# Converting float64 weights on the chip: a shift and an integer addition become one shift-and-or

## The chip, the core and the metric

The kernel runs on one core of one Trainium2 chip. The metric is the device time of one execution in microseconds, the median of several runs. A core has a matrix engine (TensorE, PE in the profile; its weight loads are PEld), a vector engine (VectorE, DVE), an activation engine (ScalarE, ACT), GpSimd (POOL), and queues that issue transfers (SyncE, SP). Each engine works through its own list of instructions in order and waits on semaphores for the others.

## The reference

Block-causal attention, then two two-layer networks, all in float32, with the networks' weights given in float64 (they come out of numpy's generator and are never cast):

```python
scores = scale * np.matmul(q, k.transpose(0, 1, 3, 2))       # 4 x 8 heads, 576 x 64
scores = np.where(block_i >= block_j, scores, -1000000000.0) # blocks of 64
scores = scores - np.max(scores, axis=-1, keepdims=True)
attn = np.exp(scores)
attn = attn / (np.sum(attn, axis=-1, keepdims=True) + 1e-09)
x = np.matmul(attn, v)            # reshaped to 2304 tokens x 512

h = x @ w_in                      # 512 -> 2048, first network
x = np.maximum(0.01 * h, h) @ w_out
h = x @ w_in2                     # 512 -> 2048, second network
out = (h * (1.0 / (1.0 + np.exp(-h)))) @ w_out2
```

## The kernel before, in words

**Stages.** The 2304 tokens are six blocks of 384. Block 0's attention comes first, with PE in full float32; then block 0 goes through the first network, again in full float32 (16 steps of a first-layer product, L1440 or L1454, and a second-layer product, L1466). In that stretch the attention of block 1 is woven in (scores L1046, products with the values L989). Blocks 1 to 5 go through the first network with operands split into a high and a low part, three products each (L1445 to L1447, L1474), with the attention of blocks 2 to 5 woven in (scores L1139, L989). The second network works on all tokens with seven products of halves in place of eight (first layer L1712 to L1714, last layer L1875); its operands are sums and differences of quarters, each split into high and low (`split`: high by L378 or L380, low by L389).

**The conversion.** The chip gets the float64 weights as 64-bit words. `convert` (L407) makes 128 x 512 of them into float32; it runs 64 times: 32 times for the first network (`first_weights`, up to about 124 us), 16 times in `first_pair` and 16 times in `last_raw` for the second (about 480 to 673 us). A transfer brings the words into a slot of the tile `raw` (three slots). Then:

- `scaled` (L425, ACT): the upper half word, read as a float32, times 2^-112, which sets the exponent right; into a tile `cy` (two slots).
- `low` (L433 on ACT or L435 on DVE): the lower half word times 2^-29, rounded to a 16-bit integer: the three mantissa bits that the upper half word does not hold. Rounding can give 8, a carry into the fourth bit. It goes into the lower 16 bits of a slot of `cc` (two slots).
- `signed` (L438, DVE): the sign bit into the upper 16 bits of `cc`.
- `shifted` (L442, DVE): `cy` shifted left by three bits, in place.
- `added` (L447, DVE): `cy` plus `cc` as 32-bit integers, into a weight tile (`w`, `l`) or into `cc`.

**What sets the order.** No order is written by hand. `Schedule` (L75) plays the tasks through once when the program is built: each task has an estimated duration on each engine that may take it, a rank (when it is due) and the tasks that it depends on. A free engine takes the ready task with the lowest rank; where two engines may take a task, the one that is free first gets it. The instructions are written out in the order in which the tasks were taken, so any changed duration or dependency can move instructions on every engine. A conversion's tasks have one rank each, and are released by the load (`t_load`) and the slots of `cy` and `cc`.

**Other lines that the text names.** L1337 to L1387 are block 0's softmax (L1366 the row maximum, L1371 the exponential, L1387 the division), L1393 the transposition of its probabilities on PE, L1344 their product with the values. L1502 is the gate behind a first layer, on ACT. L1149 and L1151 are the row maxima of blocks 2 to 5, L1157 the exponential, L1176 the low part of the probabilities. L1823 to L1833 are the sums for the last layer's operands, whose high and low parts go to `h1` and `l0` among others.

Of the kernel before, what the change touches and what calls it, by code (L numbers as in the profile page):

```python
# [11 lines left out]
I32 = mybir.dt.int32  # L12
U16 = mybir.dt.uint16
U32 = mybir.dt.uint32
I64 = mybir.dt.int64
AF = mybir.ActivationFunctionType
ALU = mybir.AluOpType
# [5 lines left out]
EPS = 1e-09  # L23
PS = 2.0**15
LEAK = 0.01
BLOCKS = (384, 384, 384, 384, 384, 384)
PLACES = (0, 3, 2, 1, 5, 4)
TOK = 256
# [183 lines left out]
def rows_of(t, n):  # L212

    runs = []
    for a in range(t, t + n, P):
        r = PLACES[a // BLOCKS[0]] * BLOCKS[0] + a % BLOCKS[0]
        if runs and sum(runs[-1][1:]) == r:
# [6 lines left out]
def head_ranges(blk, n_heads):  # L224

    pieces = []
    first = t0 = PLACES[blk] * BLOCKS[blk]
    end = first + BLOCKS[blk]
    while t0 < end:
# [10 lines left out]
def attn_mlp_mlp(  # L240
# [10 lines left out]
    nc = tc.nc  # L251
    S, H = SEQ, vL.shape[1]
    D = vL.shape[-1]
    NT, DM = out.shape
    NF = w1.shape[0]
    NC = DM // P
    NJ = (S + P - 1) // P
    NBLK = len(BLOCKS)
    assert sum(BLOCKS) == NT
    NB = max(BLOCKS)  # L260
    NB0 = BLOCKS[0]
    NC0 = NB0 // P
    scale = 1.0 / float(D) ** 0.5
# [61 lines left out]
    def cc_room(dtype):  # L325
        turn_cc[0] = (turn_cc[0] + 1) % CCS
        return area("cc", "c", U32)[:, turn_cc[0] * DM : (turn_cc[0] + 1) * DM].bitcast(dtype)

    def raw_room():

        k = turn_raw[0] = (turn_raw[0] + 1) % RAWS
        return area("raw", turn_raw[1])[:, k * 2 * DM : (k + 1) * 2 * DM]
# [9 lines left out]
    engine = {"DVE": nc.vector, "POOL": nc.gpsimd, "ACT": nc.scalar}  # L342
    plan = Schedule()


    def act(n, psum=False, pointers=0):
        return 0.833 * n + (52 if psum else 94) + 93 * pointers

    def dve(n, pointers=0):
        return Both(1.042 * n + 68 + 61 * pointers)  # L350
# [4 lines left out]
    def dve2x(n, pointers=0):  # L355
        return Both(0.521 * n + 68 + 61 * pointers)
# [10 lines left out]
    def dma(deps, rank, size, emit, issue=600, after=(), slow=0, lag=0):  # L367
        t = plan.add({"SP": issue}, deps, rank, lambda e: emit(), after)
        done = plan.add({"DMA": size / 360}, [t], rank, lambda e: None)
        done.lag = lag  # L370
        if slow:
            done, t0 = plan.add({"LATE": 1}, [done], rank, lambda e: None), done
        done.issue = t
        return done
# [32 lines left out]
    def convert(src, f, sl, rk, load_rank, to=None, slow=0, lag=0):  # L407

        d = {}
        raw_free, raw_after, raw_users = raws.next()
        cy_free, cy_after, cy_users = cys.next()
        cc_free, cc_after, cc_users = ccs.next()

        def load():
            r = raw_room().bitcast(I64)
            nc.sync.dma_start(out=r, in_=src[f, :, sl])
            d["w0"] = r.bitcast(U32).rearrange("p (n two) -> p n two", two=2)[:, :, 0]
            d["sign"] = r.bitcast(U16).rearrange("p (n four) -> p n four", four=4)[:, :, 3]  # L420
            d["top"] = r.bitcast(F32).rearrange("p (n two) -> p n two", two=2)[:, :, 1]

        def scaled(e):
            d["y"] = cy.tile([P, DM], F32, tag="cy", name="cy")
            nc.scalar.activation(d["y"], d["top"], AF.Copy, scale=2.0**-112)  # L425

        def half_words(i):
            return d["c"].bitcast(U16).rearrange("p (n two) -> p n two", two=2)[:, :, i]

        def low(e):  # L430
            d["c"] = cc_room(U32)
            if e == "ACT":
                nc.scalar.activation(half_words(0), d["w0"], AF.Copy, scale=2.0**-29)  # L433
            else:
                nc.vector.tensor_scalar(half_words(0), d["w0"], 2.0**-29, None, op0=ALU.mult)  # L435

        def signed(e):
            nc.vector.tensor_scalar(half_words(1), d["sign"], 0x8000, None, op0=ALU.bitwise_and)  # L438

        def shifted(e):  # L440
            yu = d["y"].bitcast(U32)
            nc.vector.tensor_scalar(yu, yu, 3, None, op0=ALU.logical_shift_left)  # L442

        def added(e):
            ci = d["c"].bitcast(I32)
            d["x"] = d["c"].bitcast(F32) if to is None else to
            engine[e].tensor_tensor(d["x"].bitcast(I32), d["y"].bitcast(I32), ci, op=ALU.add)  # L447

        t_load = dma(raw_free, load_rank, DM * P * 8, load, after=[*raw_after, *raw_later], slow=slow, lag=lag)
        raws.takers.append(t_load.issue)  # L450
        t_y = plan.add({"ACT": act(DM) + 50}, [t_load, *cy_free], rk, scaled, cy_after)
        cys.takers.append(t_y)
        t_w = plan.add({"DVE": dve2x(DM) + 110, "ACT": act(DM) + 150}, [t_load, *cc_free], rk, low, cc_after)
        ccs.takers.append(t_w)
        t_c = plan.add({"DVE": dve2x(DM) + 110}, [t_load], rk, signed, [t_w])
        t_t = plan.add({"DVE": dve2x(DM) + 60}, [t_y], rk, shifted)
        t_x = plan.add({"DVE": dve(DM) + 70}, [t_w, t_c, t_t], rk, added)
        raw_users += [t_y, t_w, t_c]
        cy_users.append(t_x)
        if to is not None:  # L460
            cc_users.append(t_x)
        return d, t_x, cc_users
# [9 lines left out]
    def first_weights():  # L472

        got = []
        for i in range(2 * NF):
            f, sl = i // 2, slice((i % 2) * DM, (i % 2 + 1) * DM)
            rk = CONV0 + CONV1 * f
            to = wx[f][:, sl] if f < NATIVE else None
            got.append(convert(w1, f, sl, rk, LOAD0 + RAW0 + 20 * i if i < 4 else rk - CONV_LOAD, to, slow=LATER if i < 4 else 0))
        return got  # L480
# [102 lines left out]
    def first_pair(p):  # L583

        rk = unit3(0, p) - W2_AHEAD
        d0, t0, users0 = convert(w2, 2 * p, slice(0, DM), rk, rk - CONV_LOAD, lag=LAG)
        d1, t1, users1 = convert(w2, 2 * p + 1, slice(0, DM), rk, rk - CONV_LOAD, lag=LAG)
        t_free, t_after, t_users = cys.next()
        d = {}
# [899 lines left out]
    def add_step(blk, f):  # L1489
# [9 lines left out]
        def gate1(e):  # L1499
            at = (blk * NF + f) % 2 * NB  # L1500
            s.g = gates[0][:, at : at + n]
            nc.scalar.activation(s.g, s.h[:, :n], AF.Prelu, alpha=LEAK)  # L1502

# [561 lines left out]
```

## Time and profile before

| | |
|---|---|
| runs | 912.48, 912.71, 912.92 us; median 912.71 us |
| profiled execution | 912.12 us, span from first to last instruction 910.4 us |
| PE | busy 897.8 us (99%) |
| DVE | busy 781.4 us (86%) |
| ACT | busy 542.6 us (60%) |
| POOL | busy 17.1 us (2%) |
| TensorE clock granted | 1.00 throughout |

The profile is of one execution. Its lines give, for an instruction or a group, the engine, the line of the kernel, what is written and read, the shape, the duration, and in brackets or behind a bar the idle time ahead of it with what ended it. Durations run from start to end; neighbours on DVE and ACT overlap by some 0.05 to 0.1 us, so what an instruction holds its engine for is the distance to its successor's start, called its step here.

### The profile page before, as it was taken

The page shows a single profiled execution, that of the slowest core. Times are in us where ns is not written, and L with a number is a line of the kernel's source. Part 1 is how long each engine was busy: PE and PEld are TensorE (multiplying, and loading weights), DVE is VectorE, ACT ScalarE, POOL GpSimd, SP SyncE. Part 2 cuts the span into 40 slices and gives each one's busy share as a digit, 9 for nine tenths or more (in the row PEclk, how much of TensorE's full clock was granted, in tenths as well). Part 3 has the DMA queues.
Part 4 walks back from the last instruction along what each step waited for, and adds up shares of the span by engine and source line. Part 5 has one row for each costly group of instructions (what it writes and reads, how often), then busy time and mean ns, then how long its engine had stood idle before and what let it go on. Part 6 is the DMA issues. An engine that isn't in the chain of part 4 may idle for free.

```text
span 910.4 us, 18148 instructions
## 1 busy us (share of the span) xinstructions
PE 897.8 (99%) x6569; PEld 832.0 (91%) x6569; DVE 781.4 (86%) x1802; ACT 542.6 (60%) x1195; POOL 17.1 (2%) x79
## 2 busy tenths in 40 slices
PE   9999999999999999999999999999999999999997
PEld 4655569999999999999999999999999999999997
DVE  6889899998898889888828988898899999888865
ACT  7998687776666767676627656564465632131322
POOL 0000000000000000000000000000000000000000
PEclk9999999999999999999999999999999999999999
DMA  7597827766765686856535426688755545353422
GB/s 236 179 236 191 245 89 171 143 147 151 168 162 114 151 161 145 172 157 160 105 95 197 122 82 231 230 292 290 260 192 186 180 125 161 98 159 96 148 67 86
DMA packets 176042, 149.70 MB, mean 164 GB/s; under 512 B 109264, under 2 KB 154064, under 8 KB 175952
## 3 DMA queue, kind: packets, MB, share of 16 engines
q1 hardware_dynamic: 175952, 148.55, 58.9%
q8 instruction: 51, 0.84, 0.4%
q14 instruction: 39, 0.32, 0.1%
HBM read 90.70 MB, written 32.51 MB: 135 GB/s over the span
## 4 chain that ended last, share of the span: by engine, by line
PE 86%; DVE 10%; ACT 2%; issue 1%; DVEq 0%; ACTq 0%
PE acc L1474 12%; PE acc L1875 8%; PE h L1445 5%; PE s L1875 5%; PE h L1446 5%; PE h L1447 5%; PE h L1440 4%; PE s L1139 4%; PE u L1474 4%; PE x L989 3%; PE acc L1466 3%; PE acc L1712 3%; PE acc L1713 3%; PE acc L1714 3%; PE x L1875 3%; PE u L1875 3%
## 5 line engine op out<-in xcount | busy, mean ns | idle before, releaser
L1157 ACT ACTIVATE p<-s,st 128x288 f32<-128x288 f32 (+4 forms) x120 | 62.4, 522 | 44.6 <-DVE st L1149 22.8
L1502 ACT ACTIVATE g<-h 128x384 f32<-128x384 f32 x96 | 46.8, 488 | 55.6 <-PE h L1447 49.0
L1474 PE MATMUL acc<-ghi,w 128*128 128x384 f32 x255 | 66.5, 337 | 0.0
L1139 PE MATMUL s<-k,q 128*128 128x288 f32 (+5 forms) x288 | 65.4, 322 | 0.8 <-ACT p L1157 0.8
L389 DVE TENSOR_TENSOR glo<-g,ghi 128x384 fp32r<-128x384 f32 x80 | 44.2, 552 | 24.4 <-ACT ghi L378 23.8
L1171 ACT ACTIVATE hl<-p,st 128x576 f16<-128x576 f32 (+5 forms) x93 | 55.9, 620 | 15.3 <-DVE st L1167 5.4
L1176 DVE SCALAR_TENSOR_TENSOR hl<-p,st,hl 128x576 f16<-128x576 f32 (+4 forms) x96 | 59.0, 625 | 2.8 <-ACT hl L1171 2.0
L1445 PE MATMUL h<-h,w 128*128 128x384 f32 x180 | 60.7, 337 | 0.0
L1764 ACT ACTIVATE e<-e 128x384 f32<-128x384 f32 (+1 forms) x72 | 42.7, 627 | 27.2 <-DVE e L1737 21.5
L1447 PE MATMUL h<-h,w 128*128 128x384 f32 x160 | 53.6, 335 | 0.0
L1446 PE MATMUL h<-l,w 128*128 128x384 f32 x160 | 53.6, 335 | 0.0
L1139 PEld LDWEIGHTS s<-k,q 128*128 128x128 f32 x288 | 48.0, 188 | 5.1 <-ACT p L1157 1.9
L425 ACT ACTIVATE cy<-raw 128x512 f32<-128x512 f32 x64 | 42.9, 670 | 10.6 <-DVE cc L447 4.9
L1474 PEld LDWEIGHTS acc<-ghi,w 128*128 128x128 f32 x255 | 45.6, 188 | 0.8
L378 ACT ACTIVATE ghi<-g 128x384 fp32r<-128x384 f32 x77 | 40.2, 522 | 1.2
L1474 PE MATMUL acc<-glo,w 128*128 128x384 f32 x120 | 40.2, 335 | 0.0
L1149 DVE TENSOR_REDUCE st<-s 128x1 f32<-128x320 f32 (+3 forms) x72 | 36.4, 505 | 2.4 <-PE s L1139 0.2
L989 PEld LDWEIGHTS <-vp 128*64 128x64 f16 x1296 | 31.5, 111 | 7.2 <-issue 7.2
L1445 PEld LDWEIGHTS h<-h,w 128*128 128x128 f32 x180 | 33.8, 188 | 0.2
L1440 PE MATMUL h<-h,w 128*128 128x384 f32 x96 | 33.8, 495 | 0.0
L378 ACT ACTIVATE h<-raw 128x768 fp32r<-128x768 f32 (+1 forms) x16 | 12.5, 781 | 34.8 <-PE acc L1875 30.6
L1712 PE MATMUL acc<-h,w 128*128 128x384 f32 x96 | 32.2, 335 | 1.0 <-ACT l L378 1.0
(386 smaller groups left out, 2872.1 us busy)
## 6 DMA issues: line engine op xcount, KB each, us to landing
raw<-w SPq DMA_DIRECT2D x64, 512.0 KB, 4.9
raw<-g SPq DMA_DIRECT2D x64, 256.0 KB, 3.1
g<-e SPq DMA_DIRECT2D x48, 192.0 KB, 3.1
g<-e SPq DMA_DIRECT2D x24, 384.0 KB, 3.2
kqr<-kq_l SPq DMA_DIRECT2D x16, 480.0 KB, 3.7
kqr<-kq_l SPq DMA_DIRECT2D x16, 416.0 KB, 3.8
v<-vL SPq DMA_DIRECT2D x16, 320.0 KB, 3.2
y<-yT SPq DMA_DIRECT2D x12, 384.0 KB, 3.9
```

The source lines that it names most:

```text
L989: nc.tensor.matmul(o[i * D : (i + 1) * D, c], v[i][part][:, j], p[i][a], start=start and t == 0, stop=stop and t == len(terms) - 1,)
L1139: nc.tensor.matmul(s[:, :w], hd.q[:, a : a + P], hd.k[:, k0:k1], start=i + j == 0, stop=i == len(hds) - 1 and j == 1,)
L1157: nc.scalar.activation(p[:rows, k0:k1], u.s[piece][:rows, :w], AF.Exp, bias=nm[:rows], accum_out=s2[:rows, piece : piece + 1])
L1171: nc.scalar.activation(hl[:rows, 0, :n], p[:rows], AF.Copy, scale=rc[:rows])
L1176: nc.vector.scalar_tensor_tensor(hl[:rows, 1, :n], p[:rows], rc[:rows], hl[:rows, 0, :n], op0=ALU.mult, op1=ALU.subtract)
L1440: nc.tensor.matmul(h, w[:, c * P : (c + 1) * P], x_hi[0][:, c, : s.n], start=c == 0, stop=c == NC - 1)
L1445: nc.tensor.matmul(h, w1_lo[s.f][:, sl], hi[:, c, : s.n], start=c == 0, stop=False)
L1446: nc.tensor.matmul(h, w1_hi[s.f][:, sl], lo[:, c, : s.n], start=False, stop=False)
L1447: nc.tensor.matmul(h, w1_hi[s.f][:, sl], hi[:, c, : s.n], start=False, stop=c == NC - 1)
L1474: nc.tensor.matmul(s.acc[c][:, : s.n], a, b, start=s.f == 0 and i == 0, stop=s.f == NF - 1 and i == 2)
L1712: nc.tensor.matmul(o, wlo[:, w], xhi[:, x], start=k == 0, stop=False)
L1875: nc.tensor.matmul(o, a[:, x], b, start=i == 0 and j == 0 and q == 0, stop=i == NP - 1 and q == 2, skip_group_check=True,)
```

## The change

`shifted` and `added` are replaced by one instruction, `joined`: DVE's scalar_tensor_tensor shifts `cy` left by three and ors it with `cc`. An or has no carry, so the low bits must not round up to 8: `low` now subtracts just under a half ahead of the rounding to an integer, by the activation's bias on ACT or by a second operation of the same tensor_scalar on DVE. The schedule's tasks change with it: `shifted` is gone, `joined` is entered at 601 ns (`dve(512)`) where `added` had 671 and `shifted` 395, and it waits for `scaled`, `low` and `signed` directly.

```diff
+LOW = 2.0**-29 * (1 - 2.0**-20)
...
         def low(e):
             d["c"] = cc_room(U32)
             if e == "ACT":
-                nc.scalar.activation(half_words(0), d["w0"], AF.Copy, scale=2.0**-29)
+                nc.scalar.activation(half_words(0), d["w0"], AF.Copy, scale=LOW, bias=-0.5)
             else:
-                nc.vector.tensor_scalar(half_words(0), d["w0"], 2.0**-29, None, op0=ALU.mult)
+                nc.vector.tensor_scalar(half_words(0), d["w0"], 2.0**-29, -0.50001, op0=ALU.mult, op1=ALU.add)
...
-        def shifted(e):
-            yu = d["y"].bitcast(U32)
-            nc.vector.tensor_scalar(yu, yu, 3, None, op0=ALU.logical_shift_left)
-
-        def added(e):
-            ci = d["c"].bitcast(I32)
+        def joined(e):
             d["x"] = d["c"].bitcast(F32) if to is None else to
-            engine[e].tensor_tensor(d["x"].bitcast(I32), d["y"].bitcast(I32), ci, op=ALU.add)
+            nc.vector.scalar_tensor_tensor(
+                d["x"].bitcast(U32), d["y"].bitcast(U32), 3, d["c"],
+                op0=ALU.logical_shift_left, op1=ALU.bitwise_or,
+            )
...
-        t_t = plan.add({"DVE": dve2x(DM) + 60}, [t_y], rk, shifted)
-        t_x = plan.add({"DVE": dve(DM) + 70}, [t_w, t_c, t_t], rk, added)
+        t_x = plan.add({"DVE": dve(DM)}, [t_y, t_w, t_c], rk, joined)
```

The lists of all engines change from about row 47 of DVE on. Three places show how; behind the change the kernel is two lines shorter, so a line from 450 on has a number lower by two, and those ahead of it one higher.

DVE in the middle of block 0's softmax. `small` and `e` belong to the softmax, `xw` takes transposed probabilities from PE (`pt`), and `w_158` is the first weight tile. Before:

```order
L1338 RECIPROCAL small_173<-small_173 128x4
L442 TENSOR_SCALAR cy<-cy 128x512
L1387 TENSOR_SCALAR e<-e,small_173 128x256
L1365 MEMSET s 64x64
L1366 TENSOR_REDUCE small_173<-s 128x1
L1365 MEMSET s 64x64
L1366 TENSOR_REDUCE small_173<-s 128x1
L1387 TENSOR_SCALAR e<-e,small_173 128x256 x2
L447 ISA w_158<-cy,cc 128x1024
L380 COPY xw<-pt_414 128x512
```

The same place of the changed kernel:

```order
L1336 RECIPROCAL small_173<-small_173 128x4
L443 SCALAR_TENSOR_TENSOR w_158<-cy,cc 128x512
L1385 TENSOR_SCALAR e<-e,small_173 128x256
L1363 MEMSET s 64x64
L1364 TENSOR_REDUCE small_173<-s 128x1
L1363 MEMSET s 64x64
L1364 TENSOR_REDUCE small_173<-s 128x1
L1385 TENSOR_SCALAR e<-e,small_173 128x256 x2
L439 TENSOR_SCALAR cc<-raw 128x512
L381 COPY xw<-pt_414 128x512
```

The joined instruction stands where the shift stood, ahead of two row maxima; the place of the addition goes to the next conversion's sign.

PE where block 0 enters the first network. `s<-t_152` are scores of block 1, `h` is the bank of the first layer, `w_158` and `w_159` the weights of its first two steps. Before:

```order
L1046 MATMUL s<-t_152 128x128 x2
L1454 MATMUL h<-h_314,w_158 128x128 x4
L1046 MATMUL s<-t_152 128x256 x2
L1440 MATMUL h<-h_314,w_159 128x384 x4
L1466 MATMUL acc<-g,w_158 128x384 x3
```

The same place of the changed kernel:

```order
L1044 MATMUL s<-t_152 128x128 x2
L1452 MATMUL h<-h_314,w_158 128x128 x4
L1438 MATMUL h<-h_314,w_159 128x384 x4
L1044 MATMUL s<-t_152 128x256 x2
L1464 MATMUL acc<-g,w_158 128x384 x3
```

The second step's first layer now follows the first step's at once, and the scores come after it. From the second network's first product on, PE's list is the same in both.

DVE where the last layer begins. `x`, `y` and `l` (the tile `l0`) are low parts of operands of the last layer, `w` weights of it, `e` sums. Before:

```order
L389 TENSOR_TENSOR x<-e,x 128x1024
L389 TENSOR_TENSOR y<-raw,cc 128x768
L389 TENSOR_TENSOR y<-t_6514,y 128x1024
L1823 TENSOR_TENSOR e<-raw 128x512
L389 TENSOR_TENSOR w_1703<-l,w_1703 128x256
L1829 TENSOR_TENSOR e<-e,raw 128x256
L389 TENSOR_TENSOR t<-l 128x256
L1833 TENSOR_TENSOR e<-e,raw 128x256
L654 SCALAR_TENSOR_TENSOR t<-t,l 128x256
L1823 TENSOR_TENSOR e<-raw 128x512
L380 CAST x<-raw 128x768
L389 TENSOR_TENSOR l_1785<-e,h_804 128x1024
```

The same place of the changed kernel:

```order
L390 TENSOR_TENSOR x<-e,x 128x1024
L390 TENSOR_TENSOR y<-raw,cc 128x768
L390 TENSOR_TENSOR y<-t_6468,y 128x1024
L390 TENSOR_TENSOR w_1486<-t,w_1485 128x512
L1821 TENSOR_TENSOR e<-raw 128x512
L390 TENSOR_TENSOR w_7089<-l,w_1486 128x512
L1827 TENSOR_TENSOR e<-e,raw 128x256
L661 SCALAR_TENSOR_TENSOR l<-t,l 128x256
L1831 TENSOR_TENSOR e<-e,raw 128x256
L1821 TENSOR_TENSOR e<-raw 128x512
L390 TENSOR_TENSOR xw<-raw,x 128x768
L390 TENSOR_TENSOR l_1783<-e,h_805 128x1024
```

Weights' low parts of 512 columns and the low part into `xw` now stand ahead of the low part into `l0`, and three pieces of 256 columns and a copy on DVE no longer do.

## Rows read from the trace of the kernel before

**Rows 1.** The page's first part: busy time of each engine, share, instructions.
```profile
PE 897.8 (99%) x6569; PEld 832.0 (91%) x6569; DVE 781.4 (86%) x1802; ACT 542.6 (60%) x1195; POOL 17.1 (2%) x79
```

**Rows 2.** Waits of PE and its weight loads: total us, times, longest.
```profile
PE s L1139 <- ACT p L1157: 0.8, 2, 0.5
...
PEld L989 <- issue: 7.2, 25, 0.5
```

**Rows 3.** Three stretches: busy us of PE, PEld, DVE, ACT, POOL; clock; DMA.
```profile
40.00:130.00 90.00, 90.00 (x428) 51.90 (x427) 81.30 (x229) 75.98 (x175) 1.55 (x6) 1.00 0.75 201
150.00:200.00 50.00, 49.17 (x434) 46.23 (x433) 48.22 (x134) 37.84 (x93) 3.40 (x16) 1.00 0.69 144
700.00:750.00 50.00, 49.07 (x352) 48.62 (x352) 49.07 (x85) 26.20 (x42) 0.00 (x0) 1.00 0.48 161
```

**Rows 4.** The conversion's lines: busy us, mean ns, idle before and its releasers.
```profile
L433 ACT ACTIVATE cc<-raw 128x512 uint16<-128x512 uint32 x40 | 30.9, 777 | 2.0 <-DMA w2k<-cc 2.0
L442 DVE TENSOR_SCALAR cy<-cy 128x512 uint32<-128x512 uint32 x64 | 26.3, 415 | 4.0 <-ACT cy L425 3.8
L447 DVE CUSTOM_DVE_ANT_0 cc<-cy,cc 128x1024 uint16<-128x1024 uint16 x34 | 23.3, 685 | 0.8
L435 DVE TENSOR_SCALAR cc<-raw 128x512 uint16<-128x512 uint32 x24 | 11.0, 459 | 3.0 <-DMA raw<-w 1.6 <-DMA w2k<-cc 1.0 <-DMA g<-e 0.2
```

**Rows 5.** DVE in order of time: start, duration, instruction.
```profile
155.78 0.55 DVE L389 TENSOR_TENSOR glo<-g,ghi 128x384 fp32r<-128x384 f32 x1
156.25 0.55 DVE L815 SCALAR_TENSOR_TENSOR q<-kqr,q 128x384 fp32r<-128x384 f32 x1
156.72 0.81 DVE L857 TENSOR_REDUCE vs<-v 128x1 f32<-128x640 f32 x1
```

**Rows 6.** The chain that ended last, from 23 to 28 us: start, us, what.
```profile
23.48 0.32 DVE cy L442
...
24.91 0.56 DVE small L1366
...
27.34 0.66 PE pt L1393 x4
```

**Rows 7.** PE, and one gate on ACT, in order of time.
```profile
36.46 1.16 PE L1454 MATMUL h<-h,w 128*128 128x128 f32 x8
37.59 1.46 PE L1046 MATMUL s<-t 64*128 64x256 f32 x4
38.97 2.85 PE L1440 MATMUL h<-h,w 128*128 128x384 f32 x8
...
41.86 0.49 ACT L1502 ACTIVATE g<-h 128x384 f32<-128x384 f32 x1 [0.21 <-PE h L1440]
...
56.31 0.70 PE L1046 MATMUL s<-t 64*128 64x256 f32 x4
56.94 2.85 PE L1440 MATMUL h<-h,w 128*128 128x384 f32 x8
```

**Rows 8.** DVE, and PE's wait behind it, where the last layer begins.
```profile
722.50 0.95 DVE L389 TENSOR_TENSOR h<-raw,h 128x768 fp32r<-128x768 f32 x1
...
728.12 0.95 DVE L389 TENSOR_TENSOR y<-raw,cc 128x768 fp32r<-128x768 f32 x1
728.99 1.22 DVE L389 TENSOR_TENSOR y<-t,y 128x1024 fp32r<-128x1024 f32 x1
730.12 0.68 DVE L1823 TENSOR_TENSOR e<-raw 128x512 f32<-128x512 f32 x1
730.72 0.42 DVE L389 TENSOR_TENSOR w<-l,w 128x256 fp32r<-128x256 f32 x1
731.06 0.42 DVE L1829 TENSOR_TENSOR e<-e,raw 128x256 f32<-128x256 f32 x1
...
733.47 1.22 DVE L389 TENSOR_TENSOR l<-e,h 128x1024 fp32r<-128x1024 f32 x1
...
734.74 0.39 PE L1875 MATMUL acc<-w,l 128*128 128x256 f32 x1 [0.89 <-DVE l L389]
```

## The prediction

> **What bounds the kernel now.** I read the busy shares first, then the waits of PE, then stretches, then the places where PE waited. PE is busy 897.8 of the 910.4 us of the span [rows 1]. Its busy time is modelled, so the stretches are needed beside it: from 40 to 130 us PE is busy 90.00 of 90 us, although this is where the first network's 32 conversions run and DVE has 81.30 and ACT 75.98 us of work [rows 3]. So while conversions run, PE never waits for them, and a cheaper one is worth nothing there by itself. PE's idle time sits in few places: 0.83 us between 150 and 200 us and 0.93 us between 700 and 750 us [rows 3], and the start up to about 39 us, where block 0's softmax runs through DVE and ACT and PE fills the time. Of the first, 0.8 us are two waits of score products for an exponential, whose row maxima come from a DVE that is busy 48.22 of the 50 us [rows 2, 3]; the second is one wait of 0.89 us for a low part made by DVE [rows 8]. Another 7.2 us are 25 pauses of the weight loads ahead of a group of value products, put down to issue and not to an engine [rows 2]. So the change can move the time by the start, by these waits, and by what the new lists put elsewhere.
>
> **What is removed.** 64 shifts of 415 ns [rows 4]. In the chain one holds DVE for 0.32 us [rows 6]. That is 64 x 0.32 = 20.5 us of DVE.
>
> **What replaces the addition.** The addition runs as a custom instruction over 1024 16-bit elements, 685 ns in its largest group (34; the other 30 stand at about 0.68) [rows 4]. With the overlap of some 0.09 us that the shift shows (415 ns against 0.32 on the chain) its step is 0.60. No row has a scalar_tensor_tensor with bit operations. The nearest is L815: 384 columns, both inputs four bytes wide, step 0.47 from 156.25 to 156.72, the same as the plain subtraction ahead of it, 0.47 from 155.78 to 156.25 [rows 5]. A two-input operation on 512 columns steps 0.60 (730.12 to 730.72) [rows 8]. I take 0.60, no change against the addition. The lower bound is 0.32, if two operations with two inputs went at the shift's rate; the upper one is a step of 1.13, that of 1024 columns (728.99 to 730.12) [rows 8], if each element took two passes. I stay at 0.60 because L815 also does two operations on two inputs and pays for one.
>
> [...]
>
> **The low word.** The bias or second operation is priced at nothing: it rides on an instruction that exists. On ACT the row is 777 ns [rows 4]. Above, I bound the bias by the 0.12 us that this form is over the gate's 0.49 on 384 columns, scaled to 512 (0.65) [rows 4, 7]; 31 times 0.12 is 3.8 us, hidden while ACT has 14 us free in the stretch from 40 to 130 [rows 3]. On DVE a second operation goes with the first (L815 again), and if it added a whole shift of 0.32, 33 of them would eat 10.6 of the 20.5 us. The new lists move nine low words from ACT to DVE (24 to 33), at 459 ns less 0.09 about 3.3 us. So DVE ends with some 17 us less work, ACT with 9 x 0.777 = 7 us less.
>
> **Where it touches the path.** (1) In block 0's softmax the shift at 23.48 is on the chain, ahead of the row maxima that lead to PE's transpositions at 27.34 [rows 6]. The joined instruction stands in its place: 0.60 - 0.32 = **+0.28 us**. The sign that takes the addition's place stands behind that part of the chain, and so gains nothing for 27.34. (2) At 37.59 PE runs a pair of 256-column scores that is done at 38.97, 1.38 us later; the same pair undisturbed takes 0.63 (56.31 to 56.94), so 0.75 us are a stall [rows 7]. In the new list the next step's first layer comes ahead of these scores. It overwrites the bank `h` and must wait for the gate: that starts about 0.04 us after the product's end (41.82 to 41.86) and takes 0.49 [rows 7], with some 0.05 us back to PE. From the end of L1454 at 37.62 the product then starts about 38.2, 0.60 us after the 37.59: **-0.15 us**. From there to 130 us PE has work without a gap and keeps the offset. (3) By 195 us, where the longer of the two score waits (0.5) lies, DVE has had 32 shifts less (-10.2), seven of the moved low words more (+2.6) and some 2 us of other tasks that the lists move to it: 5 to 6 us less ahead of that maximum. That wait should go; at the shorter one I count only 0.4 us less, and give it a third: **-0.6 us**. (4) The new list has 25 groups of value products where the old has 26; a pause is 7.2 / 25 = 0.29 us [rows 2]: **-0.29 us**. (5) Behind 500 us PE's order is the same in both. Where the last layer begins, DVE's queue from the low part of `h` at 722.50 starts behind results of PE's last first-layer products, so less DVE work earlier does not move it. Up to the low part of `l0` it took 10.97 us (722.50 to 733.47) [rows 8]. The new list has there, by the steps of rows 8, three of 768 columns (0.87 each), two of 1024 (1.13), six of 512 (0.60) and nine of 256 (0.33 to 0.34): 11.5 us. PE's wait of 0.89 grows: **+0.53 us**.
>
> Sum: 0.28 - 0.15 - 0.6 - 0.29 + 0.53 = -0.23. The profiled execution took 912.12 us, of which 910.4 are the span, and it lies 0.59 under the median of 912.71. So 911.9 for an execution like it, and **912.5 us** for the median. That cannot be told from no change: about 0.2%, 1.8 us, is what a measurement of this kernel can tell.
>
> **What hides the saved 17 us.** PE, which is full. If PE were not the bound from 40 to 130, a saving of 32 x 0.32 = 10 us would show there; it is covered by 90.00 us of PE work.
>
> **Rivals.**
> *The lightened DVE clears every wait that it feeds.* For it: DVE is busy 48.22 of 50 us in the one stretch and 49.07 in the other [rows 3], and the waits there end on its results. Then 0.8 + 0.89 + 0.29 go, the stall of 0.75 at 37.59 goes too, and the start costs 0.28: -2.45, 910.3 us. Against it: the gate takes the stall's place, and the queue at 722.50 hangs on PE. Chance 0.17.
> *Slower: joined goes at half rate.* Its place is each of the 64 conversions, its price a step of 1.13. It decides from a step of 0.92 on, the 0.60 + 0.32 of the pair that it replaces. At 23.48 it costs 0.81 in place of 0.28, and a second one ahead of the softmax's end up to 0.5 more. From 40 to 130 us, 32 x 0.21 = 6.7 and the moved low words' 2.6 would fill the 8.7 us that DVE has free there [rows 3], and what is left runs into the stretch from 150 to 200 with 1.8 free: 1 to 5 us of waits. 914.5 to 919, middle 916.5 us. Against it: L815. Chance 0.07. [...]
> *Slower: the new lists make new waits of the old kind.* Each row maximum that gets another task ahead of it can hold a score product for 0.4 us (0.8 over 2) [rows 2]; five more of them than the forecast has, between 130 and 480 us, make 914.5, seven 915.3. For it: almost every list changes. Against it: less DVE work, and in PE's list the scores come at nearly the same places from 160 us on. Chance 0.10.
> *That the change does not do what it says* is ruled out: the built list has one instruction in place of the two, 64 times.
>
> The forecast has 0.66, with its own range 911.0 to 914.3: the start (2) may come out 0.4 either way, (3) between 0 and -0.8, (5) between -0.3 and +1. The range to hold the time 8 times in 10 reaches down into the first rival and up to the middle of the third: 910.2 to 914.9. Faster by more than 0.2% has 0.17, within 0.66, slower 0.17.
>
> **What would show it.** Joined at a mean of 0.68 us, 64 times, and DVE's busy time some 15 to 22 us lower, show the prices right; a mean near 1.2 shows the half rate. PE's first 384-column product of the first layer (38.97 now) should start at 38 to 39.2, and PE busy 90 of 90 from 40 to 130 again. The scores' wait for the exponential should be 0.5 or less in all, and the wait for the low part in `l0` about 1.4. The prediction is wrong if PE shows waits for weights (`w`) or new waits for exponentials of over 1.5 us together, or if the start moves by over 1 us.

## The result, and the profile after

The changed kernel takes 918.01 us (median of four executions, 916.47 to 918.71), the one before 912.82 (912.48 to 913.04): a ratio of 1.0054 (95% interval 1.0042 to 1.0067). It is 5.2 us slower; the forecast was 912.5 us in a range of 910.2 to 914.9. The profiled execution took 917.65 us with a span of 915.7, which is 5.3 more than the 910.4 of before.

The first part of the page of the changed kernel, which answers [rows 1]:

```profile
PE 900.4 (98%) x6569; PEld 832.6 (91%) x6569; DVE 769.7 (84%) x1759; ACT 533.7 (58%) x1170; POOL 17.5 (2%) x83
```

DVE has 11.7 us less (some 17 were forecast) and ACT 8.9 less (7), so work did go. The conversion's lines (as in rows 4; L426 makes `cy`, L443 is joined):

```profile
L426 ACT ACTIVATE cy<-raw 128x512 f32<-128x512 f32 x64 | 42.9, 672 | 18.8 <-DMA raw<-w 13.6 <-DVE vs L877 1.3 <-DVE st L1055 1.2
...
L434 ACT ACTIVATE cc<-raw 128x512 uint16<-128x512 uint32 x31 | 23.9, 776 | 0.0
...
L443 DVE SCALAR_TENSOR_TENSOR cc<-cy,cc 128x512 uint32<-128x512 uint32 x34 | 23.3, 687 | 1.3
...
L436 DVE TENSOR_SCALAR cc<-raw 128x512 uint16<-128x512 uint32 x33 | 15.2, 461 | 7.4 <-DMA raw<-w 5.6 <-DMA w2k<-cc 1.6
```

Joined costs 687 ns where the addition cost 685 [rows 4], and the low word 776 and 461 where it cost 777 and 459: every price held. New is what stands at the right: before `cy`, ACT waits 13.6 us for loads of weights (4.4 before the change), and DVE 5.6 before `cc` (1.6 in rows 4).

The three stretches of [rows 3]:

```profile
40.00:130.00 90.00, 89.16 (x426) 51.14 (x425) 79.05 (x225) 73.97 (x175) 0.97 (x5) 1.00 0.80 202
150.00:200.00 50.00, 49.72 (x440) 47.81 (x442) 46.31 (x139) 35.77 (x90) 4.29 (x19) 1.00 0.70 148
700.00:750.00 50.00, 48.45 (x327) 48.04 (x326) 47.02 (x80) 25.80 (x41) 0.00 (x0) 0.97 0.45 148
```

In the first PE is no longer full, in the second it waits less (the forecast's third term), and in the third it waits more and its granted clock is not 1.00. Waits of PE and its weight loads, by what they waited for (after [rows 2]):

```profile
PEld L987 <- issue: 7.5, 25, 0.5
...
PE h L1438 <- ACT g L1500: 1.1, 2, 0.7
PE acc L1873 <- DVE l L390: 1.0, 1, 1.0
...
PE h L1443 <- ACT g L1500: 0.8, 1, 0.8
...
PE s L1137 <- ACT p L1155: 0.6, 3, 0.2
PE acc L1873 <- ACT h L379: 0.6, 1, 0.6
```

The waits for a gate (L1500) are new, and so is that of 0.6 us for `h` (0.05 before). The gate's first stands at the start, where the forecast had it under (2); the second, and the one of L1443, stand where it had none:

```profile
38.53 2.85 PE L1438 MATMUL h<-h,w 128*128 128x384 f32 x8 [0.69 <-ACT g L1500]
...
123.55 1.88 PE L1438 MATMUL h<-h,l 128*128 128x384 f32 x5 [0.43 <-ACT g L1500]
```

The last of the gate's, and ACT's list ahead of it, in order of time:

```profile
143.58 0.65 ACT L379 ACTIVATE w<-l 128x512 fp32r<-128x512 f32 x1
144.10 0.55 ACT L379 ACTIVATE ghi<-g 128x384 fp32r<-128x384 f32 x1
144.52 0.65 ACT L379 ACTIVATE w<-l 128x512 fp32r<-128x512 f32 x1
148.59 1.15 ACT L379 ACTIVATE l<-cc 128x512 fp32r<-128x512 f32 x2 [3.42 <-DVE w L390]
149.64 0.47 ACT L1500 ACTIVATE g<-h 128x384 f32<-128x384 f32 x1
...
150.17 0.44 PE L1443 MATMUL h<-h,e 128*128 128x384 f32 x1 [0.76 <-ACT g L1500]
```

The gate at 149.64 stands behind two copies of converted weights, these behind a wait of 3.42 us, and PE waits for the gate. PE's last product into `h` ahead of this gate had ended at 147.27 us (start 146.94, 0.33 long), 2.37 us before the gate started: it was ACT's list ahead of it that made it late. (A wait in brackets counts from the modelled end of the product before. Counted from the time at which the next product would have followed it is some 0.15 us longer; so the expectations below have 0.74 and 1.11 us for the two waits of 0.60 and 0.95 at the last layer's start.)

Where the last layer begins (as in rows 8), first DVE, then PE:

```profile
725.85 0.95 DVE L390 TENSOR_TENSOR h<-raw,h 128x768 fp32r<-128x768 f32 x1
...
737.36 1.21 DVE L390 TENSOR_TENSOR l<-e,h 128x1024 fp32r<-128x1024 f32 x1
...
737.18 0.39 PE L1873 MATMUL acc<-xw,h 128*128 128x256 f32 x1 [0.60 <-ACT h L379]
738.63 0.39 PE L1873 MATMUL acc<-w,l 128*128 128x256 f32 x1 [0.95 <-DVE l L390]
```

From the low part of `h` to that of `l0` it now takes 11.51 us (725.85 to 737.36), where 11.5 were forecast. What no part of the forecast had is TensorE's clock behind these two waits (columns: length, PE busy, granted clock, DMA share, GB/s):

```profile
737.00:739.00 2.00, 0.87 (x5) 1.00 0.77 224
739.00:743.00 4.00, 4.00 (x24) 0.57 0.86 257
743.00:745.00 2.00, 2.00 (x19) 1.00 0.19 65
```

In the single microseconds from 739 on the granted clock is 0.71, 0.50, 0.50 and 0.58, which makes 3.4 us at 0.50. In them a product of 256 columns is followed by the next after 0.21 us (739.44 to 739.65), ahead of them and behind after 0.12 (739.09 to 739.21, 743.09 to 743.21).

The 5.3 us, by the times of the same products: by 42 us PE is 0.39 behind (one of L1464's products at 42.37, before 41.98). At the last layer's wait it is 3.89 behind (738.63 against 734.74 [rows 8]), of which 0.6 come from the longer waits there. So some 2.9 us are lost between, net of what was won at the scores, and 1.4 behind it, where the clock falls.

### The profile page after: what moved, and what is told of

Same layout as the page of the kernel before. It is cut to its first block, busy times and chain, and to the rows that moved or that the text cites. A ratio compares the mean times of both kernels' runs of the same rounds, so it can differ in the third digit from the quotient of the medians.

```text
span 915.7 us, 18100 instructions
## 1 busy us (share of the span) xinstructions
PE 900.4 (98%) x6569; PEld 832.6 (91%) x6569; DVE 769.7 (84%) x1759; ACT 533.7 (58%) x1170; POOL 17.5 (2%) x83
## 4 chain that ended last, share of the span: by engine, by line
PE 82%; DVE 11%; DMA 3%; ACT 2%; issue 1%; SPq 0%; DVEq 0%; ACTq 0%
PE acc L1472 13%; PE acc L1873 8%; PE h L1443 6%; PE h L1444 6%; PE h L1445 6%; PE s L1873 5%; PE s L1137 4%; PE u L1472 4%; PE x L987 3%; DMA raw<-w 3%; PE acc L1710 3%; PE acc L1711 3%; PE acc L1712 3%; PE u L1873 3%; PE x L1873 3%; PE s L1711 2%
## 5 line engine op out<-in xcount | busy, mean ns | idle before, releaser
L1500 ACT ACTIVATE g<-h 128x384 f32<-128x384 f32 x96 | 46.8, 487 | 45.7 <-PE h L1445 44.2
L1443 PE MATMUL h<-h,w 128*128 128x384 f32 x180 | 60.7, 337 | 0.0
L426 ACT ACTIVATE cy<-raw 128x512 f32<-128x512 f32 x64 | 42.9, 672 | 18.8 <-DMA raw<-w 13.6
L1443 PEld LDWEIGHTS h<-h,w 128*128 128x128 f32 x180 | 33.8, 188 | 0.3
```

Source lines behind the costliest of these rows:

```text
L1443: nc.tensor.matmul(h, w1_lo[s.f][:, sl], hi[:, c, : s.n], start=c == 0, stop=False)
```

## Experiments: the instruction apart from the order

Two kernels complete the square. The first has the joined instruction and the new low word in the lists of before (the planner still has a task for the shift, which emits nothing):

```diff
         def shifted(e):
-            nc.vector.tensor_scalar(yu, yu, 3, None, op0=ALU.logical_shift_left)
+            pass
...
         def added(e):
...
-            engine[e].tensor_tensor(d["x"].bitcast(I32), d["y"].bitcast(I32), ci, op=ALU.add)
+            nc.vector.scalar_tensor_tensor(..., 3, d["c"], op0=ALU.logical_shift_left, op1=ALU.bitwise_or)
```

> The lists of before on every engine, with the joined instruction standing where the addition stood, no shift, and the low word without rounding: the work of the change without its order. Theory of the lists (the loss is made by the new order, not by the instruction): 911.5 to 913.0 us, PE busy 90.00 of 90 us from 40 to 130 us, granted clock 1.00 to the end. Rival, the instruction (joined or the new low word hold DVE, ACT or a port so that others run later): 916 to 918.5 us with the waits for gates between 100 and 160 us as after the change.

The second has the lists of the changed kernel and the old instructions, the old low word too:

```diff
         def joined(e):
...
-            nc.vector.scalar_tensor_tensor(..., 3, d["c"], op0=ALU.logical_shift_left, op1=ALU.bitwise_or)
+            nc.vector.tensor_scalar(yu, yu, 3, None, op0=ALU.logical_shift_left)
+            nc.vector.tensor_tensor(d["x"].bitcast(I32), d["y"].bitcast(I32), d["c"].bitcast(I32), op=ALU.add)
```

> The lists of the changed kernel, with shift and integer addition back to back where joined stood, and the low word rounded as before: the order of the change without its work. Theory of the lists: 917 to 920 us (the changed kernel's loss, and up to 2 us more, since DVE has 20 us of work that the lists do not know), with PE waiting for gates between 100 and 160 us. Rival, the instruction: 912 to 913.5 us.

Measured, medians in us:

| | old instructions | joined |
|---|---|---|
| lists of before | 913.05 (before, 21 executions) | 911.81 (0.9987, 0.9978 to 0.9996) |
| lists of the change | 922.90 (1.0106, 1.0091 to 1.0122) | 918.01 (1.0054, 1.0042 to 1.0067) |

The instruction is a gain in either list, 1.2 and 4.9 us. The order costs 6.2 us with it and 9.9 without. The second kernel lies 2.9 us above its range: with DVE's unplanned 20 us it takes 4.9 more than the changed kernel, where 2 were allowed for. The rival, that the instruction does the harm, falls. In the first kernel the stretches read:

```profile
40.00:130.00 90.00, 90.00 (x428) 51.90 (x427) 73.25 (x202) 75.89 (x175) 1.56 (x6) 1.00 0.76 200
150.00:200.00 50.00, 49.14 (x434) 46.12 (x433) 48.23 (x135) 37.85 (x94) 3.42 (x16) 1.00 0.70 143
700.00:750.00 50.00, 49.07 (x354) 48.63 (x353) 49.12 (x85) 25.86 (x42) 0.00 (x0) 1.00 0.47 156
```

From 40 to 130 us DVE has 8 us less to do than in [rows 3] and PE is as full as it was: the cover that the forecast named is there, in this order. In the second row PE's waits stand where they were, so they did not hang on DVE's load ahead of them. What is won lies at 30 us, where PE's wait of 0.6 us for `xw` goes.

## Experiments: other lists

Is it this list, or any new one? Three kernels change one number that only the planner reads, one of them in the kernel before, and one tells the planner of later loads:

```diff
# joined at the pair's price
-        t_x = plan.add({"DVE": dve(DM)}, [t_y, t_w, t_c], rk, joined)
+        t_x = plan.add({"DVE": dve(DM) + 465}, [t_y, t_w, t_c], rk, joined)
# joined 30 ns dearer
+        t_x = plan.add({"DVE": dve(DM) + 30}, [t_y, t_w, t_c], rk, joined)
# the kernel before, addition 10 ns dearer
-        t_x = plan.add({"DVE": dve(DM) + 70}, [t_w, t_c, t_t], rk, added)
+        t_x = plan.add({"DVE": dve(DM) + 80}, [t_w, t_c, t_t], rk, added)
# loads of the first network 2 us later, from the fifth on
-            got.append(convert(..., slow=LATER if i < 4 else 0))
+            got.append(convert(..., slow=LATER if i < 4 else 0, lag=0 if i < 4 else 2000))
```

> The changed kernel with one number other: the planner is told that joined takes as long as shift and addition did together (465 ns more). Instructions are those of the change, the lists are new again. If the lists went wrong because the planner now thinks DVE lighter and lays ACT's and PE's work tighter: 911.5 to 913.5 us, PE without waits for gates. If any new list of these 32 conversions is as likely to lose as that of the change: anywhere from 911 to 919 us, with waits of its own at other places.

> The changed kernel, its instructions untouched; the planner alone is told that joined takes 30 ns more, and all lists come out new. If each list is a draw: anywhere from 914 to 925 us, with waits of its own. If the loss of the changed kernel follows from the lighter conversions: 917 to 919 us, with the waits for gates between 110 and 155 us.

> The kernel before, its instructions untouched; the planner alone is told that the addition takes 10 ns more, and all lists come out new. If a new list as such is a draw that mostly loses against that of before: 914 to 922 us. If lists lose only where conversions grew lighter: 912.5 to 913.5 us.

> The changed kernel with one number other: the planner is told that the conversions' loads of the first network (from the fifth on) arrive 2 us later than it thought. If late loads (ACT 13.6 us and DVE 5.6 us idle until a load, against 4.4 and 1.6 before) heap the copies in front of the gates at 120 to 130 us: the two waits for gates there go (1.9 us), and 915.5 to 916.5 us are left. If the loads only follow a late order of conversions: no better than 917.5 us, and waits as long at other places.

Measured: 922.10 us at the pair's price, 915.67 with 30 ns more, 924.59 for the kernel before with 10 ns more (ratio 1.0125, 1.0111 to 1.0139), 914.97 with the later loads. Four new lists, and all lose, the last by least (1.0016, 1.0007 to 1.0025), each at places of its own. At the pair's price PE waits 2.2 us for a converted weight (`w`, L443) at 99.84. In the kernel before with its 10 ns it is this:

```profile
PE s L1139 <- DVE k L389: 4.6, 1, 4.6
```

Two of the four lie above the range given for a draw, by 3.1 us (the pair's price) and 2.6 (10 ns more), and the theories under which these two would lose nothing fall. So a new list is a draw, and all five drawn here lose against the one that the kernel had; why that one is better than all five, no run shows. The draw of the later loads did what was expected of it in the first part, and its time is 0.5 us below the range given: PE is busy 90.00 of 90 us from 40 to 130 and 20.00 of 20 from 130 to 150, and ACT waits 2.5 us for loads, none of it before 150 us. Its waits where the last layer begins are those of the change.

## Experiment: the late loads

The lists of the changed kernel stay word for word; the loads of the first network carry half the columns from the fifth on, and the conversions read old values in the other half:

```diff
+        late_one = src is w1 and len(raws.users) > 3
...
-            nc.sync.dma_start(out=r, in_=src[f, :, sl])
+            m = DM // 2 if late_one else DM
+            nc.sync.dma_start(out=r[:, :m], in_=src[f, :, sl.start : sl.start + m])
```

> The changed kernel, lists untouched, with only the first half of the columns loaded in each load of the first network's weights from the fifth load on (the conversions work on old values in the other half): the loads carry half the bytes. If late loads are what makes PE wait for gates between 110 and 155 us: these waits go (1.2 us for gates, 0.4 to 0.7 for scores), 915.8 to 916.8 us, and ACT's idle time until a load falls from 13.6 us to under 4. If the heaped copies stand in the order itself: ACT waits less for loads, but PE waits for the gate at 150 us as before, 917.3 to 918.2 us.

Measured: 913.39 us (912.66 to 915.29, 11 executions), 4.6 less than the changed kernel and more than either theory gave. PE at the product that waited at 150.17:

```profile
146.50 0.34 PE L1474 MATMUL u<-glo,y 128*128 128x384 f32 x1
146.68 0.37 PE L1445 MATMUL h<-h,e 128*128 128x384 f32 x1
```

It comes 3.49 us earlier and without a wait. PE's order is the same in both, so the two can be laid beside each other product by product: the run starts 0.2 us behind at 38.53, and its lead grows by 0.7 at the scores of 70.23 to 70.92, 0.7 at those of 119.58, 0.6 at the gate of 123.55, 0.4 at the scores of 135.93 and 0.9 at the gate of 150.17 (times of the changed kernel), the rest in steps of about 0.1; at 737.18 it is 3.59. The rest of the 5.0 us between the two spans (910.7 and 915.7) is the clock, which stayed up behind the last layer's start in this execution (1.00 from 735 to 739 us). The copies still stand ahead of the gates. They do no harm when they are on time. ACT's idle time for loads fell to 7.2 us, not under 4, so that number missed; of the 7.2, 3.3 lie in the first network, whose loads alone were halved (10.9 in the changed kernel).

How a late load becomes a late gate shows in the chain that ends in the product at 150.17 (start, us, what):

```profile
109.88 0.38 DVE cc L439
...
110.31 5.86 DMA raw<-w
...
116.25 0.68 ACT cy L426
...
123.12 0.37 ACT g L1500
...
148.59 1.15 ACT l L379 x2
149.74 0.39 ACT g L1500
...
150.17 0.44 PE h L1443
```

The load goes out when DVE has read an earlier conversion's sign, which frees a slot of `raw`, and lands 5.86 us later. ACT stands still until then and is busy from there to the gate at 123.12, the one that PE waits 0.43 us for. From 125 to 148.6 us the chain runs through DVE, and from it to the copies and the gate at 149.74. ACT's waits for loads from 40 to 150 us, before the change and after it (and the wait of 3.42 us seen above):

```profile
ACT cy L425 <- DMA raw<-w: 3.2, 2, 3.0
...
ACT cy L426 <- DMA raw<-w: 10.9, 9, 2.2
ACT l L379 <- DVE w L390: 3.4, 1, 3.4
```

Nearly all of the 10.9 us lie from 56 to 75 us and from 108 to 117, ahead of the places where the run with half loads gains.

The loads themselves are not slower: from issue to landing the 21st to the 32nd take 5.0 us on average in either kernel, although the DMA engines are fuller (busy shares of 1.02, 1.01 and 0.99 in the three stretches of 10 us from 80 us on, 0.72, 1.05 and 0.81 before). The planner, which thinks the conversions lighter, takes them earlier: the 23rd load is issued at 83.4 us (90.3 before), and its joined instruction starts at 93.2 (the addition at 101.8 before). For a load it reckons in both kernels with 600 + 1456 + 1500 ns, 3.6 us from issue to use (`dma` and `HOP` in the code). A conversion that stands ahead of its load waits, and what is queued behind it, copies and gates, comes late. That the planner's 3.6 us put it there is argued from the code; the run with the later loads, which adds 2 us to them and has no wait of ACT for loads before 150 us, agrees. The 28 half loads land after 3.4 us (median; 5.0 for the whole loads of the same network in the changed kernel). With them the DMA engines are emptier for every other transfer too (busy share 0.56 from 40 to 130 us, 0.80 in the changed kernel), so that run does not tell by itself whether a conversion's own load or one beside it was the late one; the chain above goes through a conversion's own. That it is the transfers and not the order by itself, the run does tell. Why the old list, planned with the same 3.6 us, suffers less, is not shown.

## Experiments: the last layer's start and the clock

The high and low part of `h` there are made in two pieces, 256 and 768 columns, so that PE's first products wait for 256 columns alone; lists stay. This stands on the changed kernel, on the old lists with joined, and on the list of the later loads:

```diff
+            cuts = [slice(0, n), slice(n, m)] if (g, i) == (0, 2) and m == 4 * n else [slice(0, m)]
...
+                for c in cuts:
+                    copy(e, parts()[0][:, c], value()[:, c])
...
```

> The changed kernel with the lists as they are, but where the last layer begins the high and the low part of h are made in two pieces (256 and 768 columns), so that PE's next products wait for 256 columns alone. By the sum of this document the waits of 0.74 and 1.11 us shrink by 0.4 and 0.6 or more. If the fall of the clock behind them hangs on them, it goes too, 1.6 us: 915.2 to 916.2 us, clock 0.998 or higher. If it has another cause: 916.8 to 917.3 us and the clock as low as before (0.995 to 0.998).

> The lists of before with the joined instruction (911.81 us), and the two pieces of h at the last layer's start as in the run above. The version that should beat both kernels: PE's waits there, 0.2 and 1.05 us, shrink to about 0.5 in all, so 911.0 to 911.4 us. If PE then waits as long for the rest of the low part, no gain: 911.8 us.

> The kernel whose planner knows the loads 2 us later (914.97 us, granted clock 0.995 to 0.998 in 8 of 11 executions), and at the last layer's start the high and low part of h in two pieces, as in the run before with the changed kernel's lists. If the clock there falls because the two waits lie so close together (0.75 and 1.11 us): 912.4 to 913.4 us, clock 0.999 or 1.000 in nearly all executions. If the gain with the changed kernel's lists was an accident of its order: 914.3 to 915 us, clock as low as without the pieces.

Measured on the changed kernel: 915.61 us (914.14 to 916.60), clock 0.999 or 1.000 in all seven executions, where the changed kernel had 0.995 to 0.998 in its four. PE has one wait there:

```profile
737.13 0.39 PE L1883 MATMUL acc<-w,l 128*128 128x256 f32 x1 [1.01 <-DVE l L390]
```

The wait for the high part (0.60) is gone, the one for the low part is not, so 0.6 of the 2.4 us are the wait's. Of the 1.8 left, 1.4 is what was lost behind this place with the clock; 0.4 stay open. With the later loads: 914.97 to 913.27 us, 1.7 for the same 0.6, and the clock at 0.998 or above in 11 of 11 executions (before that in 5 of 11, 0.995 to 0.997 in the others). On the old lists, whose clock had not fallen: 911.61 us, no difference from 911.81 that can be told. The low part's wait went from 0.89 to 0.39 us, and PE then waits 0.56 us at 764.61 for DVE. DVE is the limit in this stretch (busy 49.12 of 50 us from 700 to 750 in the old lists with joined) and takes the gain back.

The other way round, to see whether longer waits bring the clock down there, the old lists with joined and longer work at that place (a copy of 512 columns ahead of the high part, a subtraction of 256 ahead of the low):

```diff
-            hi = plan.add(copy_on(m), deps, r, lambda e: copy(e, parts()[0], value()))
...
+            def high(e):
+                if (g, i) == (0, 2) and m == 4 * n:
+                    copy(e, parts()[0][:, : 2 * n], value()[:, : 2 * n])
+                copy(e, parts()[0], value())
...
```

> Lists of before with the joined instruction (911.81 us), and where the last layer begins the high part of h is preceded by a copy of its first 512 columns on ACT (0.52 us) and its low part by a subtraction of 256 columns on DVE (0.33), so that PE's pair of waits there grows from 0.2 and 1.05 us to about the 0.74 and 1.11 of the changed kernel. [...]

Measured: 912.08 us, clock 0.998 to 1.000. One wait of 1.35 us stood there and not the pair that was meant (the first wait did not grow), so the run tells only that a single wait of 1.35 us left the clock up here. And the changed kernel, started later:

```diff
-            for i in range(WARM):
+            for i in range(WARM + 15):
```

> The changed kernel with 15 more of the matrix products that fill PE at the start (15 x 0.427 = 6.4 us), so that the last layer begins 6 us later in the run, about where it begins in the run with the old instructions in the new lists, whose clock stayed at 1.00 behind the same two waits. If the clock's fall depends on where in the run the waits lie: 921.5 to 923 us, clock 0.999 or 1.000. If it hangs on the waits and the work around them alone: 924 to 925 us, clock 0.995 to 0.998 as in the changed kernel.

Measured: 918.03 us, and neither theory as it was put. Of the 6.4 us, 3.6 are left at the first layer's product (42.13 against 38.53) and 2.6 at the gate of 150.17 and behind it. The executions fall into two groups: four of 917.36 to 918.38 us with a clock of 0.999 or 1.000, two of 921.46 and 921.85 us with 0.995. Nothing lies between, so what goes with the clock is worth 3.1 to 4.5 us there. The profiled one is of the second group:

```profile
553.00:556.00 3.00, 1.75 (x8) 1.00 0.98 294
556.00:559.00 3.00, 3.00 (x12) 0.50 0.99 333
...
743.00:747.00 4.00, 4.00 (x23) 0.59 0.91 277
```

The clock falls twice here, and the first fall is behind two waits (0.96 and 0.58 us, where the second network begins) that the changed kernel has too, with its clock at 1.00. All profiled executions of this document have them, and the clock falls behind them in this one and in that of joined 30 ns dearer (0.76 from 552 to 555 us) alone. The pair of waits at the last layer's start stands in the run with half loads (1.0 and 0.6 us) and in the second kernel of the square (0.61 and 0.95) as well, and there the clock stays, at 1.00 from 735 to 739 us with half loads, and in the second kernel:

```profile
743.00:745.00 2.00, 0.61 (x3) 1.00 0.55 163
745.00:749.00 4.00, 4.00 (x34) 1.00 0.86 280
```

So two short waits close together are not enough. Nor are two needed: at the pair's price the clock falls behind a single wait, of 1.30 us for an exponential at 73.49, with no other in the 16 us before it:

```profile
72.00:75.00 3.00, 1.70 (x6) 1.00 1.01 223
75.00:79.00 4.00, 4.00 (x8) 0.57 0.19 48
```

What decides between the executions stays open.

## Why the prediction was wrong, point by point

- **Prices.** Right: joined 687 ns, the low word unchanged. DVE's relief was over-estimated: 11.7 us in place of some 17, and below the 15 to 22 that were to show the prices right. Joined alone takes 18.0 off (763.4 us busy in the old lists); the new lists give DVE nine more low words, as forecast, and copies of other kinds. The rival at half rate falls (it asked for a step of 1.13, and the chain shows 0.58); that its 914.5 to 919 us hold the measured time is chance. In this trace a shift and an or on two 4-byte sources of 512 columns take 687 ns, the addition 685.
- **The start, (1) and (2).** +0.13 was forecast, 0.39 came. Joined stands in the chain at 23.56 us with 0.58 where the shift had 0.32, as forecast; the first layer's product started at 38.53 and not at 38.97 [rows 7], but the scores behind it gave that back.
- **"From there to 130 us PE has work without a gap and keeps the offset."** This is the step that failed. That a lighter DVE costs nothing there was read from the old list and is true of it (90.00 of 90 with joined in the old lists). The new list takes conversions up to 8 us earlier, their loads take 5.0 us as before, and ACT stands 10.9 us for them up to 130 us (3.2 before). PE waits for the gates and scores queued behind: it is busy 89.16 of the 90 us, and some 2.9 us are lost up to the last layer, 3.5 by the run with half loads. That run shows that the transfers are the cause; the one with the later loads, another list, agrees.
- **(3), the score waits.** -0.6 was forecast; PE's idle time from 150 to 200 us fell from 0.83 to 0.28, of which 0.17 are the end of the wait at 150.17. The reason given was wrong: with joined in the old lists DVE has 8 us less ahead of them and the waits stay. The new order moved them.
- **(4), one pause less.** Did not come: 25 pauses, 7.5 us (7.2 in rows 2).
- **(5), the last layer's start.** +0.53 forecast, 0.6 measured, and the queue's 11.5 us came out (11.51). But the wait that grew is the one for the high part (0.05 to 0.60), and the low part's, which was to reach about 1.4, is 0.95 (0.89 before): both stand behind the same queue, and PE came to the second one later. That the clock would fall behind it, 1.4 us, was in no term.
- **Rivals.** That the lightened DVE clears every wait falls: in the old lists it clears none of those named. That new lists make new waits was the right direction at a chance of 0.10. It had the kind wrong (scores behind row maxima, 0.4 each, instead of gates behind late conversions) and the size (914.5 to 915.3).

## What to carry to other kernels

Where a planner orders the work, an edit is two edits: price the instruction in the old order, then ask what the new order does, and run the instruction in the old lists before judging it. Here it is worth -1.2 us in the old order, and that kernel (911.81 us) beats both. A task that the planner thinks lighter is taken earlier, and its input takes as long as before (here a load's 5.0 us): compare, load by load, when it lands with when the new list wants it, and look at what is queued behind. The busy share of an engine that was full under the old list says nothing about the new one (PE from 40 to 130 us: 90.00 of 90 before, 89.16 after).

## What the runs showed of the hardware

TensorE's clock can fall behind short waits: in the changed kernel, behind two of 0.60 and 0.95 us, 1.45 us apart, the granted clock stood at 0.50 for 3.4 us, and 1.4 us were lost, more than the 0.6 by which the waits had grown. Behind a single wait it fell in one run (1.30 us, joined at the pair's price) and stayed up in another (1.35 us, old lists with longer work at the last layer). It fell in some executions of a kernel and not in others (with the later start two of six have the lower clock, 0.995, and are 3.1 to 4.5 us longer than the other four). What decides it, no run here shows.
